# Attention times values on TensorE: four parts of 32 columns in place of two of 64

## The chip, the cores and the metric

The kernel runs on one core of a Trainium2 chip. The metric is device microseconds of one execution. A profiled execution gives, beside its time, a trace of every instruction on the engines: TensorE (PE for matmuls, PEld for its weight loads), VectorE (DVE), ScalarE (ACT), GpSimd (POOL) and SyncE (SP, which here only issues transfers).

## The reference, cut to what matters

Two blocks follow one another: an attention in which a query sees only the keys of its own hash bucket, and a feed-forward layer.

```python
# q, k, v: (4, 8, 768, 64) f32; proj: (64, 6)
q_bits = (np.einsum('bhsd,dk->bhsk', q, proj) > 0).astype(np.int64)   # k_bits alike
q_bucket = np.sum(q_bits * powers, axis=-1)                           # 64 buckets
mask = q_bucket[:, :, :, None] == k_bucket[:, :, None, :]
scores = np.where(mask, scale * np.matmul(q, k.transpose(0, 1, 3, 2)), -1000000000.0)
attn = np.exp(scores - np.max(scores, axis=-1, keepdims=True))
attn = attn / (np.sum(attn, axis=-1, keepdims=True) + 1e-09)
out = np.matmul(attn, v)                  # the change is in this product
...
x = out.transpose(0, 2, 1, 3).reshape(B * S, H * D)                   # (3072, 512)
h = x @ w_in                              # w_in (512, 2048)
g = h * (1.0 / (1.0 + np.exp(-1.702 * h)))
return (g @ w_out).astype(np.float32)     # w_out (2048, 512)
```

## The kernel before, in words

The 32 attention heads are worked off as 16 **pairs**: `pairs` holds (batch, head pair), and the two heads j = 0, 1 of a pair share every tile. S = 768 positions are T = 6 tiles of P = 128, D = 64 is the head's width, and the queries are split into two halves c = 0, 1 of HS = 384.

All score work has keys on partitions and queries along the free axis. For pair n:

- `scores(n, c, kts)` (L423 to L433): for each key tile kt one PSUM tile `ps` gets, for each head, a bfloat16 matmul of hash features (`qf`, `kf`) and a float32 matmul of `kT` and `qT`. Each contracts over the 64 rows of its head and has 128 output partitions, so both heads use one half of the array's rows each (form 64\*128 in the profile). ACT then writes exp of it to `es[c]` (L433). `es[c]` has 385 columns per key tile and head: a last column holds a tiny constant.
- `values(n, c, kts)` (L450 to L464), the function of the change: for each key tile t and head j a float32 matmul with `vt[:, t, j, :]` (128 keys x 64) as weights and `es[c][:, t, j, :]` (128 keys x 385) as the moving operand, summed over the six key tiles into partitions 64 j to 64 j + 63 of `av`. Weights of 64 columns use one half of the array's columns (form 128\*64).
- `unload` (L471): ACT moves `av` into `xT`, the transposed input of the feed-forward, and adds the last column's value.
- `hashed` (L402 to L409) projects q and k of a later pair on the hash directions: four float32 matmuls with 32 weight columns each, 128 rows contracted, 384 moving columns, into the partition quarters of one PSUM tile (form 128\*32, L408).
- `total` (L477 to L484) sums the exponentials over the partitions with a matrix of ones: four float32 matmuls of the same shape (L484), from `acc`, which POOL (L440, L441) and DVE (L446, L448) have summed over the key tiles.
- `turn` (L388 to L391) transposes a later pair's k and q into `kT` and `qT` on DVE. These have two buffers, so pair n + 2 overwrites what the scores of pair n read.

The order of the work is written out by hand (L530 to L609) for TensorE, DVE, ACT and POOL. From pair 2 on TensorE does for each pair: the scores of both halves, the values of both halves, `hashed(n + 2)`, `total(n)`. Pairs 14 and 15 have no `hashed`; pair 1 has one before its values as well; pair 0 is split into smaller pieces. Between them DVE also converts parts of `w_in` (`convert`, L158) and inverts and applies the sums (L490 to L504).

TensorE's matmuls on float32 appear in the trace as two passes, each with a weight load of its own: where the program has one instruction, the trace has two loads and two matmuls.

The feed-forward (L693 on) comes behind, first L722, then L834, with products of matrix quarters; the change does not touch it. Last there is a second version of the whole computation (L998 on) that only runs when a value is too large; it is not run here.

Of the kernel before, what the change touches and what calls it, by code (L numbers as in the profile page):

```python
# [38 lines left out]
def kernel(  # L39
# [17 lines left out]
    nc = tc.nc  # L57

    loader = [nc.sync]
    B, H, S, D = q.shape  # L60
# [3 lines left out]
    T = S // P  # L64
# [218 lines left out]
    def attention(ff):  # L283
# [4 lines left out]
        with actx:  # L288
# [11 lines left out]
            es = [ep.tile([P, T, 2, HS + 1], F32, name=f"e{i}") for i in range(2)]  # L300
# [149 lines left out]
            def values(n, c, kts):  # L450
                if 0 in kts:


                    if c and n == 0 or c and n + 2 > last:
                        avs[n, c] = mps.tile([P, HS + 1], F32, tag="m", name="av")
                    elif c:
                        avs[n, c] = sps.tile([P, 2, 512], F32, tag="s", name="av1")[:, 0, 0 : HS + 1]
                    else:
                        avs[n, c] = aps.tile([P, HS + 1], F32, tag="av", name="av")
                av, vt = avs[n, c], vts[n]  # L460
                for t in kts:
                    for j in range(2):
                        nc.tensor.matmul(av[D * j : D * (j + 1), :], vt[:, t, j, :], es[c][:, t, j, :],  # L463
                                         start=(t == 0), stop=(t == T - 1))  # L464

            def x_of(n):
                b, hp = pairs[n]
# [71 lines left out]
            turn(1, "k")  # L539
            measure(1, "k")  # L540
            values(0, 0, low)
            fetch(2, "k")
            scores(0, 1, low)
            add_low(0, 1)
            add_high(0, 0)
            turn(1, "q")
            measure(1, "q")
            values(0, 0, high)
            unload(0, 0)
            hashed(1)  # L550
# [3 lines left out]
            scores(0, 1, high)  # L554
            measure(2, "k")
            values(0, 1, low)
            values(0, 1, high)
            unload(0, 1)
# [476 lines left out]
```

## Time and profile before

| what | us |
|---|---|
| median of 4 runs | 871.52 (871.29 to 872.07) |
| the profiled execution | 872.09 |
| its span, first to last instruction | 870.3 |
| PE busy | 860.0 |
| L463, values: 768 passes, busy | 128.2 (mean of one 0.488) |
| L432, scores, float32: 768 passes, busy | 155.1 (mean 0.482) |
| L484, sums: 128 passes, busy | 13.3 (mean 0.488) |
| L408, hash: 120 passes, busy | 25.2 (mean 0.498) |
| first matmul of the feed-forward (L722) at | 318.8 |

The busy time of a group is the time in which at least one of its instructions runs, put down to the engine, so 768 passes of 0.488 us with a busy time of 128.2 us say that several run at a time. The ends of matmuls are modelled; the starts are what to read, and the distance of two starts is the pace. In a line such as "299.31 0.85 PE L484 MATMUL dn<-acc,ones 128\*32 128x384 f32 x8" the columns are the start, the duration of the merged group, engine, line, operation, output<-inputs, rows\*columns of the array, the moving operand, and how many instructions were merged. "PEldq" is the queue from which TensorE's loads and matmuls come; its semaphore instructions tell when it passed a point of the program.

### The profile page before, as it was taken

The numbers are of one execution on the slowest core, as the hardware profiler recorded it, in microseconds if no ns is written. First come the engines' busy times: TensorE is split into PE (matmuls) and PEld (weight loads), VectorE is DVE, ScalarE is ACT, GpSimd is POOL, SyncE is SP. The second block draws the span as 40 slices with busy tenths as digits, with TensorE's granted clock in tenths as the row PEclk, the third lists the DMA queues.
The fourth block names the chain that finished last, engine by engine and source line by source line (L and its number), as shares of the span: only waits on it lengthen the run. The fifth ranks groups of instructions, "written<-read, shape, count | busy, mean of one in ns | idle before, by whom it ended". The sixth has DMA issues, their size and how long they took to land.

```text
span 870.3 us, 11937 instructions
## 1 busy us (share of the span) xinstructions
PE 860.0 (99%) x4077; PEld 503.0 (58%) x4077; DVE 722.6 (83%) x1020; ACT 313.4 (36%) x519; POOL 312.6 (36%) x275
## 2 busy tenths in 40 slices
PE   9999999999999999999999999999999999999996
PEld 5444444444444444444444444444888888888885
DVE  4589999999999897778777778888888977897786
ACT  5866667777666643322233222332000000000000
POOL 4242223324323466665543344659903100000000
PEclk9999999999999999999999999999999999999998
DMA  5537544445762204555455555575844685467524
GB/s 129 92 53 116 99 87 84 84 87 109 109 99 64 62 2 177 186 206 204 176 188 184 203 182 204 185 251 175 305 163 159 198 246 198 163 207 243 194 98 99
DMA packets 169156, 132.00 MB, mean 152 GB/s; under 512 B 123616, under 2 KB 138112, under 8 KB 163712
## 3 DMA queue, kind: packets, MB, share of 16 engines
q1 hardware_dynamic: 166528, 129.70, 51.8%
q10 hardware_dynamic: 2560, 1.46, 0.8%
q8 instruction: 34, 0.56, 0.3%
q14 instruction: 34, 0.28, 0.1%
HBM read 79.69 MB, written 50.33 MB: 149 GB/s over the span
## 4 chain that ended last, share of the span: by engine, by line
PE 97%; DVE 2%; issue 0%; ACTq 0%; ACT 0%; DVEq 0%
PE product L722 33%; PE product L834 27%; PE ps L432 18%; PE av L463 15%; PE hash L408 1%; PE dn L484 1%; DVE xT L838 1%; PE tp L366 1%; DVE y L814 1%; PE warm L359 0%; PE hash L373 0%; DVE v L838 0%; DVE raw_g L220 0%; DVE t2a L221 0%; ACTq L821 0%
## 5 line engine op out<-in xcount | busy, mean ns | idle before, releaser
L433 ACT ACTIVATE e<-ps 128x768 f32<-128x768 f32 x192 | 151.3, 812 | 28.0 <-PE ps L432 25.5
L432 PE MATMUL ps<-qT,kT 64*128 64x384 f32 x768 | 155.1, 482 | 0.0
L722 PE MATMUL product<-xT,w_in_sb 128*128 128x512 f32 x288 | 135.4, 592 | 0.0
L463 PE MATMUL av<-e,v 128*64 128x385 f32 x768 | 128.2, 488 | 0.0
L440 POOL TENSOR_TENSOR acc<-e 128x768 f32<-128x768 f32 x32 | 50.3, 1573 | 197.0 <-ACT e L433 177.5
L730 ACT ACTIVATE c<-c 128x512 f32<-128x512 f32 x72 | 45.4, 630 | 186.7 <-issue 78.7
L463 PEld LDWEIGHTS av<-e,v 128*64 128x64 f32 x768 | 54.1, 136 | 71.6 <-issue 70.1
L722 PEld LDWEIGHTS product<-xT,w_in_sb 128*128 128x128 f32 x288 | 54.6, 190 | 69.0 <-issue 64.5
L432 PEld LDWEIGHTS ps<-qT,kT 64*128 64x128 f32 x768 | 68.0, 187 | 38.6 <-issue 38.5
L722 PE MATMUL product<-t_x,s_in 128*128 128x512 f32 x192 | 90.2, 592 | 0.0
L219 POOL TENSOR_TENSOR v<-c,u 128x512 f32<-128x512 f32 x24 | 34.2, 1424 | 122.8 <-ACT c L730 122.8
L847 ACT COPY u<-product 128x256 f32<-128x256 f32 x21 | 7.8, 373 | 172.1 <-PE product L834 138.9
L722 PEld LDWEIGHTS product<-t_x,s_in 128*128 128x128 f32 x192 | 36.5, 190 | 45.9 <-issue 43.3
L432 PE MATMUL ps<-qf,kf 64*128 64x384 bf16 x384 | 62.8, 324 | 0.1
L441 POOL TENSOR_TENSOR acc<-acc,e 128x768 f32<-128x768 f32 x32 | 55.7, 1741 | 2.5
L446 DVE SCALAR_TENSOR_TENSOR acc<-e 128x768 f32<-128x768 f32 x32 | 48.8, 1525 | 5.1 <-ACT e L433 5.1
L722 PE MATMUL product<-xT,s_in 128*128 128x512 f32 x96 | 45.1, 592 | 0.0
L722 PE MATMUL product<-t_x,w_in_sb 128*128 128x512 f32 x96 | 45.1, 592 | 0.0
L432 PEld LDWEIGHTS <-kf 64*128 64x128 bf16 x384 | 18.9, 94 | 35.1 <-DMA q<-in_q_dram 6.2
L448 DVE TENSOR_TENSOR acc<-acc,e 128x768 f32<-128x768 f32 x32 | 34.4, 1076 | 3.3
L834 PE MATMUL product<-raw_g,xT 128*128 128x256 f32 x152 | 35.1, 379 | 0.0
L448 DVE TENSOR_TENSOR acc<-acc,acc 128x768 f32<-128x768 f32 x32 | 31.0, 969 | 4.8 <-POOL acc L441 1.6
(207 smaller groups left out, 1499.1 us busy)
## 6 DMA issues: line engine op xcount, KB each, us to landing
raw_g<-g_dram SPq DMA_DIRECT2D x22, 1024.0 KB
s_in<-g_dram SPq DMA_DIRECT2D x20, 1024.0 KB
g_dram<-c SPq DMA_DIRECT2D x72, 256.0 KB
g_dram<-t SPq DMA_DIRECT2D x48, 256.0 KB
raw<-in_moe_w_in_dram SPq DMA_DIRECT2D x16, 512.0 KB
raw<-in_moe_w_out_dram SPq DMA_DIRECT2D x16, 512.0 KB
v<-in_v_dram SPq DMA_DIRECT2D x32, 192.0 KB
g_dram<-u SPq DMA_DIRECT2D x24, 256.0 KB
```

Of the source, the lines that this page charges most:

```text
L219: return [lambda: eng.tensor_tensor(t1, b12, b11, op=Alu.subtract), lambda: eng.tensor_tensor(b12, b22, b12, op=Alu.subtract), lambda: eng ...
L366: nc.tensor.matmul(tp[D * j : D * (j + 1), i * P : (i + 1) * P], x[name][:, j, c * GT + i, :], ident, start=True, stop=True)
L432: nc.tensor.matmul(ps[:, j, 0:HS], a[hs, keys], m[hs, cols], start=not last, stop=last)
L433: nc.scalar.activation(es[c][:, kt, :, 0:HS], ps[:, :, 0:HS], Act.Exp, scale=1.0 / D**0.5)
L440: nc.gpsimd.tensor_tensor(acc, es[c][:, 0, :, 0:HS], es[c][:, 1, :, 0:HS], op=Alu.add)
L441: nc.gpsimd.tensor_tensor(acc, acc, es[c][:, 2, :, 0:HS], op=Alu.add)
L446: nc.vector.scalar_tensor_tensor(acc, e[0], T * TINY, e[1], op0=Alu.add, op1=Alu.add)
L448: nc.vector.tensor_tensor(acc, acc, x, op=Alu.add)
L463: nc.tensor.matmul(av[D * j : D * (j + 1), :], vt[:, t, j, :], es[c][:, t, j, :], start=(t == 0), stop=(t == T - 1))
L722: nc.tensor.matmul(ps, wq[LEFT[i]][:, kc, :], xq[RIGHT[i]][:, kc, :], start=(kc == 0), stop=(kc == K2 - 1))
L730: nc.scalar.activation(c, c, Act.Gelu_apprx_sigmoid)
L834: nc.tensor.matmul(ps, wq[LEFT[i]][:, c, :], gq[RIGHT[i]][:, c, :], start=(c == 0), stop=(c == F4 - 1))
```

## The change

`values` issues, for each key tile and head, two matmuls of 32 weight columns in place of one of 64. Their outputs are the two 32-partition quarters of the head's half of `av`. The moving operand is the same for both, 385 columns; first and last key tile open and close the sum as before. Two matmuls per key tile become four, 384 become 768, in passes 768 become 1536, each with its load.

```diff
                 for t in kts:
+
                     for j in range(2):
-                        nc.tensor.matmul(av[D * j : D * (j + 1), :], vt[:, t, j, :], es[c][:, t, j, :],
-                                         start=(t == 0), stop=(t == T - 1))
+                        for d in range(0, D, 32):
+                            nc.tensor.matmul(av[D * j + d : D * j + d + 32, :], vt[:, t, j, d : d + 32], es[c][:, t, j, :],
+                                             start=(t == 0), stop=(t == T - 1))
```

The lines behind it move by two: the matmul is L465 in the kernel after, `total`'s is L486, the feed-forward's are L724 and L836.

## The prediction

> **What bounds the kernel now.** I read the page first: the busy shares (part 1) and the chain that ended last (part 4).
>
> ```profile
> PE 860.0 (99%) x4077; PEld 503.0 (58%) x4077; DVE 722.6 (83%) x1020; ACT 313.4 (36%) x519; POOL 312.6 (36%) x275
> PE 97%; DVE 2%; issue 0%; ACTq 0%; ACT 0%; DVEq 0%
> PE product L722 33%; PE product L834 27%; PE ps L432 18%; PE av L463 15%; PE hash L408 1%; PE dn L484 1%; DVE xT L838 1%; PE tp L366 1%; DVE y L814 1%; PE warm L359 0%; PE hash L373 0%; DVE v L838 0%; DVE raw_g L220 0%; DVE t2a L221 0%; ACTq L821 0%
> ```
>
> TensorE is the path, and the changed line, L463, is 15% of it. The waits view for PE lists one wait, 1.2 us at the start. So a nanosecond saved or lost between two matmuls of the attention moves the end by a nanosecond, as long as nobody else becomes late. Each float32 matmul shows as two passes: L463 has 768 records for 16 pairs x 2 halves x 6 key tiles x 2 heads = 384 matmuls.
>
> Next the PE timeline of one period, pair 13 (a period is 19.14 us):
>
> ```profile
> 272.25 7.99 PE L463 MATMUL av<-e,v 128*64 128x385 f32 x48
> 280.17 0.52 PE L408 MATMUL hash<-kT,pf_k 128*32 128x384 f32 x2
> 280.18 0.52 PE L408 MATMUL hash<-qT,pf_q 128*32 128x384 f32 x2
> 280.51 0.49 PE L408 MATMUL hash<-kT,pf_k 128*32 128x384 f32 x2
> 280.53 0.49 PE L408 MATMUL hash<-qT,pf_q 128*32 128x384 f32 x2
> 280.84 0.83 PE L484 MATMUL dn<-acc,ones 128*32 128x384 f32 x8
> 281.60 0.34 PE L432 MATMUL ps<-qf,kf 64*128 64x384 bf16 x2
> ```
>
> and the weight loads inside the value stage (columns: start, us, engine, what):
>
> ```profile
> 310.09 0.20 PEld L463 LDWEIGHTS av<-e,v 128*64 128x64 f32 x4
> 310.46 0.14 PEld L463 LDWEIGHTS av<-e,v 128*64 128x64 f32 x2 [0.18 <-issue]
> 310.79 0.14 PEld L463 LDWEIGHTS av<-e,v 128*64 128x64 f32 x2 [0.18 <-issue]
> 311.11 0.14 PEld L463 LDWEIGHTS av<-e,v 128*64 128x64 f32 x2 [0.18 <-issue]
> ```
>
> The reader is to see three things. The 64-column parts already run two at a time: every 0.323 us a group of two starts. Lines L408 and L484 are already what the change makes of L463: four parts of 32 columns, 128 rows, 384 moving columns. Their four matmuls start within 0.02 us, the second passes 0.34 us later, and dn follows hash after 0.32 us. And between the last value group and hash there is more: the instruction starts give 0.426 us from the last L463 group (279.742) to the first L408 matmul (280.168).
>
> **The change, part by part.**
>
> *The pace inside the stage: no change.* Per key tile, 4 passes two at a time are 2 groups; 8 passes four at a time are 2 groups too. A group of two with 385 columns takes 0.323 us, a group of four with 384 columns 0.322 (hash to dn). 192 key tiles x 2 groups, 0 us each. Each load of 32 columns takes 0.109 us (L408), of 64 columns 0.136 (L463); both lie under a group, so the shorter load gains nothing here. So the naive gain of twice the parallelism is nothing: half of the array's columns was never idle.
>
> *The switch of tile shape behind the stage: gone.* Wherever consecutive stages have different shapes (64\*128, 128\*64, 128\*32, 128\*128), the last matmul to the next start is 0.41 us: 0.412 scores to av, 0.414 av to hash or dn, 0.42 dn to scores. Where the shape stays (hash to dn) it is 0.303, group start to group start 0.323. With 32 columns av, hash and dn have one shape. By group starts 0.426 becomes 0.323: 0.103 us. The value stage is followed by hash in pairs 0 to 13 and by dn in pairs 14 and 15: 16 x 0.103 = 1.65 us. In pair 1 hash also runs ahead of the value stage; that switch goes too: 0.11 us.
>
> *The first load behind a switch.* A stage that follows a switch waits for its first weights: dn takes 0.785 us to the next stage after av (pair 14), 0.761 after hash; 0.024 us. Saved 16 times: 0.38 us. At the start of the value stage the second group comes 0.374 us after the first with 64 columns; after the same switch from the scores, dn of pair 0 with 32 columns shows 0.347: 0.027 us less, in 17 starts 0.46 us; in pair 1, without the switch, 0.05 us.
>
> *Added work.* 384 more matmuls, that is 768 more loads and 768 more passes on PE's queue; the planned order of all other engines stays as it was, and no wait is added. A group of four starts 0.02 us deep in place of 0.012, so where scores follow av directly (twice, in pair 0) some 0.01 us is lost each: 0.03 us.
>
> Sum: 1.65 + 0.11 + 0.38 + 0.46 + 0.05 - 0.03 = 2.6 us less. The profiled execution took 872.09 us, 870.3 of them its span, so it would be 869.5; the median of the runs shown is 871.52, 0.57 below it, so I say 871.52 - 2.6 = **868.9 us**, 0.30% less. About 0.2%, 1.74 us, is what a measurement of this kernel can tell from no change.
>
> *What is late next.* A period gets 0.103 + 0.024 + 0.027 = 0.154 us shorter. DVE has in it:
>
> ```profile
> 213.92 0.96 DVE L448 TENSOR_TENSOR acc<-acc,acc 128x768 f32<-128x768 f32 x1
> 214.95 0.98 DVE L391 STREAM_TRANSPOSE kT<-k 128x768 f32<-128x768 f32 x1
> 215.85 0.94 DVE L391 STREAM_TRANSPOSE qT<-q 128x768 f32<-128x768 f32 x1
> ```
>
> DVE's instructions, where no semaphore instruction stands between, start some 0.08 us before the one ahead ends (215.85 against 214.95 + 0.98); only at L391 of kT, whose buffer the scores must have left, is there a gap of 0.07. So DVE waits 0.15 to 0.16 us per period for PE, just what is taken away. It stays even, or it falls behind by hundredths; its deadline, the last sum of L448 ahead of dn, ends 2.15 us before dn starts (221.27 against 223.42). Twelve periods cannot eat that. In the first feed-forward products the sum of L213 that the second product loads ends on POOL at 318.02, and that load starts at 320.18; POOL's sums hang on the scores and shift with them. Transfers for q, k and v are fetched two or three pairs ahead.
>
> *The issue rate: the unknown.* Inside the stage PE's queue must now deliver 16 instructions per key tile (8 loads, 8 passes) in 0.647 us: **40 ns each**, against 81 now. No stage of before sustains that. Bounds from rows: hash and dn together start 32 instructions in 1.01 us, 32 ns each, but from a queue that the slower value stage had filled (its semaphore instruction for dn passed at 278.14, some 34 instructions ahead of what was running). The better row is the beginning:
>
> ```profile
> L366 PEldq EVENT_SEMAPHORE  x1: 51/51/51, 3.7 to 3.7; - x1
> L373 PEldq EVENT_SEMAPHORE  x2: 51/51/51, 7.3 to 8.6; - x2
> ```
>
> Between the wait ahead of L366 (3.676) and the first wait of L373 (7.316) the queue took in all 48 loads and 48 passes of L366: 96 in 3.64 us, at most 38 ns each, and it was held back by matmuls at 53 ns each, so it can be faster. From above, the nearest row is the 51 ns of a semaphore instruction on that queue. Take 51 and a key tile costs 16 x 51 = 816 ns, +0.169 us x 192 = +32 us; take 38 and it is 0. I take 38, since it is measured on the same kind of instructions.
>
> [...]
>
> **The rivals.**
>
> A. *The queue does not keep up* (slower). For: 40 ns has never been sustained here over 16 key tiles; the 38 ns are over 96 instructions, a value stage has 384. Against: those 38 ns are an upper bound. It decides from 40 ns on: each ns above costs 16 x 192 = 3.1 us. At 51 ns: 871.5 + 32 - 2.6 = 901 us. A variant with the same sign: the queue looks only so far ahead that two parts run together once the filled queue is used up; then a tile costs 4 groups, +0.65 us x 192 = +124 us, 993 us. Hash and dn, 4 groups of four in a row, speak against it.
>
> B. *The gap is a wait, not a switch* (no change). For: the waits view puts hash's load down to DVE, "PEld hash L408 <- DVE bits L182: 7.2, 12, 0.6". Then only the shorter first loads remain, about 0.5 us: 871.0. Against: it is the same 0.60 us idle of the loads ahead of dn in pair 15, which the view calls issue; a wait for DVE would vary.
>
> C. *DVE becomes the bound.* If its 0.16 us are not slack and 2.15 us not a cushion, the twelve middle periods give nothing: 2.6 - 12 x 0.154 = 0.8 us less, 870.7.
>
> **Chances and range.** Forecast 0.74 (868.0 to 869.7: half a drain more or less, the run's own 0.3 us), B 0.05, C 0.06, A 0.15. B and C lie within 0.2%, so faster 0.74, same 0.11, slower 0.15. The range runs from 868.0 to 871.2, which takes in B and C and leaves out A, less than 2 in 10.
>
> **What would show it.** Right: the timeline has L465 with x96 per value stage of 7.78 us in place of 7.92 (23 x 0.323 + 0.347), dn always 0.76, a period of 18.99 us, loads in fours every 0.323 us, L391 of kT starting without a gap. Wrong by A: groups further apart than 0.33 us after the first two key tiles. Wrong by B: 0.41 us still stands between L465 and L408. Wrong by C: dn's loads wait for DVE's L448.

## The result, and the profile after

| | us |
|---|---|
| after, median of 40 runs | 869.83 (868.99 to 872.62) |
| before, median of 60 runs beside them | 871.40 (870.82 to 872.73) |
| ratio to before, with its 95% interval | 0.9983 [0.9979, 0.9988] |
| the profiled execution of after, and its span | 868.76, 866.9 |
| the same kernel measured twice more | 869.11 and 869.31; ratios 0.9978 [0.9968, 0.9987] and 0.9976 [0.9966, 0.9986] |

The kernel became 1.6 to 2.1 us faster by the medians, 0.17% to 0.24%, where 2.6 us were forecast. 869.83 us lies in the range, but above the forecast's own band of 868.0 to 869.7 us: the range goes on to 871.2 because it takes in rivals B and C. The two repeats lie in the band. Three things are to be separated: what the attention gained, what it lost again in one place, and what varies from run to run ahead of it.

The page of after, parts 1 and 4:

```profile
PE 856.4 (99%) x4845; PEld 499.2 (58%) x4845; DVE 719.4 (83%) x1020; ACT 313.3 (36%) x519; POOL 313.6 (36%) x275
PE 95%; DVE 3%; issue 0%; DMA 0%; ACTq 0%; ACT 0%; DVEq 0%
```

TensorE has 768 passes more and is busy 3.6 us less. The chain passes through DVE a little more often; its DVE lines are those of the feed-forward, whose first and last matmul stand 542.5 us apart in both kernels.

The PE timeline of the period of pair 13, of after:

```profile
269.39 7.97 PE L465 MATMUL av<-e,v 128*32 128x385 f32 x96
277.17 0.49 PE L408 MATMUL hash<-kT,pf_k 128*32 128x384 f32 x2
277.19 0.49 PE L408 MATMUL hash<-qT,pf_q 128*32 128x384 f32 x2
277.50 0.49 PE L408 MATMUL hash<-kT,pf_k 128*32 128x384 f32 x2
277.51 0.49 PE L408 MATMUL hash<-qT,pf_q 128*32 128x384 f32 x2
277.82 0.83 PE L486 MATMUL dn<-acc,ones 128*32 128x384 f32 x8
278.58 0.34 PE L432 MATMUL ps<-qf,kf 64*128 64x384 bf16 x2
```

By the starts the value stage takes 277.17 - 269.39 = 7.78 us (before 7.92), hash 0.65 (before 0.67), dn still 0.76. From the last matmul of L465 to hash there are now 0.298 us, before 0.414: without a change of shape the longer gap is gone. The period is 18.99 us, before 19.14.

The weight loads inside a value stage of after (start, us, engine, what; the bracket is idle time before):

```profile
306.92 0.16 PEld L465 LDWEIGHTS av<-e,v 128*32 128x32 f32 x8
307.27 0.13 PEld L465 LDWEIGHTS av<-e,v 128*32 128x32 f32 x4 [0.19 <-issue]
307.59 0.13 PEld L465 LDWEIGHTS av<-e,v 128*32 128x32 f32 x4 [0.19 <-issue]
307.92 0.13 PEld L465 LDWEIGHTS av<-e,v 128*32 128x32 f32 x4 [0.20 <-issue]
```

Loads come in fours, 0.32 us apart as the twos did, with 0.19 us of nothing between them. The pace is set by the moving columns (half of the columns take half of the time, 0.163 us, in two experiments below), and the queue keeps up.

DVE in a period of after, the lines that answer to the first two of before:

```profile
211.50 0.96 DVE L448 TENSOR_TENSOR acc<-acc,acc 128x768 f32<-128x768 f32 x1
212.54 0.98 DVE L391 STREAM_TRANSPOSE kT<-k 128x768 f32<-128x768 f32 x1
```

211.50 + 0.96 to 212.54 is 0.08 us: the gap ahead of kT, which the prediction called DVE's wait for PE and expected to close, is still there.

**The attention by itself.** From the first hash matmul (L373) to the first feed-forward matmul PE takes 309.98 us in both profiles of before and 307.51 to 307.54 in the three of after: 2.47 us less in the first of them, and nearly the same in every profile. I call this stretch the attention below and read the experiments from it, since their differences are mostly too small for medians.

### The profile page after: what moved, and what is told of

Read it like the earlier page. It is cut to its first block, busy times and chain, and to the rows that moved or that the text cites. A ratio compares the mean times of both kernels' runs of the same rounds, so it can differ in the third digit from the quotient of the medians.

```text
span 866.9 us, 13473 instructions
## 1 busy us (share of the span) xinstructions
PE 856.4 (99%) x4845; PEld 499.2 (58%) x4845; DVE 719.4 (83%) x1020; ACT 313.3 (36%) x519; POOL 313.6 (36%) x275
## 4 chain that ended last, share of the span: by engine, by line
PE 95%; DVE 3%; issue 0%; DMA 0%; ACTq 0%; ACT 0%; DVEq 0%
PE product L724 33%; PE product L836 26%; PE ps L432 18%; PE av L465 15%; PE dn L486 1%; PE hash L408 1%; DVE y L816 1%; DVE xT L840 1%; PE tp L366 0%; DVE t_x L840 0%; DMA k<-in_k_dram 0%; PE hash L373 0%; DVE t2a L221 0%; DVE raw_g L220 0%; DVE v L840 0%
## 5 line engine op out<-in xcount | busy, mean ns | idle before, releaser
L724 PE MATMUL product<-xT,w_in_sb 128*128 128x512 f32 x288 | 135.5, 593 | 0.0
L465 PE MATMUL av<-e,v 128*32 128x385 f32 x1536 | 128.0, 487 | 0.0
L724 PEld LDWEIGHTS product<-xT,w_in_sb 128*128 128x128 f32 x288 | 54.8, 190 | 68.9 <-issue 64.4
L465 PEld LDWEIGHTS av<-e,v 128*32 128x32 f32 x1536 | 48.6, 109 | 76.1 <-issue 74.5
L724 PE MATMUL product<-t_x,s_in 128*128 128x512 f32 x192 | 90.2, 593 | 0.0
L724 PEld LDWEIGHTS product<-t_x,s_in 128*128 128x128 f32 x192 | 36.6, 190 | 45.8 <-issue 43.2
L441 POOL TENSOR_TENSOR acc<-acc,e 128x768 f32<-128x768 f32 x32 | 55.9, 1746 | 2.5
L446 DVE SCALAR_TENSOR_TENSOR acc<-e 128x768 f32<-128x768 f32 x32 | 47.7, 1491 | 5.1 <-ACT e L433 5.1
L724 PE MATMUL product<-xT,s_in 128*128 128x512 f32 x96 | 45.1, 592 | 0.0
L724 PE MATMUL product<-t_x,w_in_sb 128*128 128x512 f32 x96 | 45.1, 593 | 0.0
L836 PE MATMUL product<-raw_g,xT 128*128 128x256 f32 x152 | 35.1, 379 | 0.0
```

The costliest lines, as they stand in the source:

```text
L441: nc.gpsimd.tensor_tensor(acc, acc, es[c][:, 2, :, 0:HS], op=Alu.add)
L446: nc.vector.scalar_tensor_tensor(acc, e[0], T * TINY, e[1], op0=Alu.add, op1=Alu.add)
L465: nc.tensor.matmul(av[D * j + d : D * j + d + 32, :], vt[:, t, j, d : d + 32], es[c][:, t, j, :], start=(t == 0), stop=(t == T - 1))
L724: nc.tensor.matmul(ps, wq[LEFT[i]][:, kc, :], xq[RIGHT[i]][:, kc, :], start=(kc == 0), stop=(kc == K2 - 1))
L836: nc.tensor.matmul(ps, wq[LEFT[i]][:, c, :], gq[RIGHT[i]][:, c, :], start=(c == 0), stop=(c == F4 - 1))
```

## The experiments

Theory **switch**: the pace inside a stage is the same for two parts of 64 and four of 32, and the gain comes from changes of shape between stages that go away. Rivals: **parts**, each value stage is cheaper by itself with 32 columns; **queue**, the rate of issue costs or nearly costs something; later **DVE**, the sums come too late in pair 1; and **start**, the first transfer lands later.

### Both kernels once more

No edit, beside the first two experiments on the same chip.

> The kernel before once more, as a control. Theory 'start': L373 to L722 is 309.98 us again, the first L373 matmul lies anywhere from 7.9 to 9 us. Theory 'body': the body is the one that varies. Ratio 1.000 with an interval that shows what this comparison can tell, about 0.0005 to either side.

> The changed kernel once more. Open after its first profile: that profile is 3.4 us shorter in span than the one of before, 2.47 of it from the first L373 matmul to the first feed-forward matmul and 0.85 ahead of L373, while the medians lie only 1.6 us apart. Theory 'start': the stretch ahead of L373 (8.81 us in the profile of before, 7.96 in that of after) differs from run to run, the 2.47 us behind it do not; then this profile shows 307.5 us from L373 to L724 again (within 0.1) whatever its start is, and a start anywhere from 7.9 to 9 us. Theory 'body': runs other than the profiled one lose up to 1 us in waits of the attention; then 307.5 becomes up to 308.5 in this profile, with gaps that a wait explains. Ratio to before about 0.998 in both.

Measured: before_again 871.25 us, ratio 1.0002 [0.9993, 1.0011], attention 309.98 us; after_again 869.11 us, 0.9978 [0.9968, 0.9987], attention 307.54 us. The gain is there again, and the attention repeats to 0.03 us while the point at which it starts does not: 7.61 and 9.09 us here, 8.81 and 7.96 in the first profiles.

### Only one of the two halves in parts of 32

```diff
-                        for d in range(0, D, 32):
+                    w = 32 if c else D      # second_half_32; first_half_32: D if c else 32
+                        for d in range(0, D, w):
```

> Only the products of the second query half (c = 1) are in 32-column parts, those of the first half stay at 64. Theory 'switch' (the gain is the change of tile shape between the value stage and hash or dn): the switch only moves into the middle of the value stage, from between av and hash to between the two halves; hash follows av after 0.32 us, but 0.41 us and a late second group appear between the halves. Net within 0.1 us of the kernel before from L373 to the feed-forward (309.9, before 309.98), ratio 0.9995 to 1.0005. Rival 'parts' (narrower parts are cheaper in themselves): half of the gain, 1.2 us, ratio 0.9986.

> Only the products of the first query half (c = 0) are in 32-column parts. Theory 'switch': a switch is added in the middle of the value stage of 15 pairs (0.10 us, and 0.05 for the late second group) and none is removed, except the one behind the first half of pair 0 and the one between hash and av of pair 1; the shorter first load gives 0.03 us back per pair. 15 x 0.12 - 0.3 = 1.5 us slower than before from L373 to the feed-forward (311.5), ratio 1.001 to 1.002. Rival 'parts': 1.2 us faster, ratio 0.9986.

Measured: second_half_32 871.42 us, ratio 1.0002 [0.9993, 1.0011], attention 309.96 us (0.02 less than before). first_half_32 873.51 us, 1.0026 [1.0016, 1.0036], attention 311.99 us (2.01 more). The PE timeline of pair 13 in second_half_32:

```profile
272.00 8.12 PE L465 MATMUL av<-e,v 128*64 128x385 f32 x72
279.94 0.49 PE L408 MATMUL hash<-kT,pf_k 128*32 128x384 f32 x2
```

and in first_half_32:

```profile
273.74 8.12 PE L465 MATMUL av<-e,v 128*32 128x385 f32 x72
281.79 0.52 PE L408 MATMUL hash<-kT,pf_k 128*32 128x384 f32 x2
```

The merged line carries the shape of its first matmul; inside it the shape changes once. In second_half_32 the stage takes 7.94 us: the gap ahead of hash is now 0.299 us in place of 0.414, yet the stage with its change of shape inside is 0.02 us longer than before, so what the gap lost has come back within the stage, and what hash wins (0.643 in place of 0.669 us, thirteen times) is lost there too. In first_half_32 there are two changes of shape, in the middle and ahead of hash, and the stage takes 8.05 us, 0.137 us more than before. **Parts** wanted both kernels faster, about half the gain each; it falls. **Switch** has both signs. Its size in first_half_32 was put at +1.5; of the 2.01 measured, 1.76 are switches with the late loads behind them, and 0.25 are pair 1's dn, of which more below.

### How fast can the queue deliver?

Each product is cut into 192 and 193 moving columns, so that a key tile needs twice as many loads and passes for the same columns; once with parts of 32 (pieces_32: 32 instructions per key tile), once with parts of 64 (pieces_64: 16 instructions).

```diff
-        nc.tensor.matmul(av[...], vt[...], es[c][:, t, j, :], start=(t == 0), stop=(t == T - 1))
+        for s in ((0, 192), (192, HS + 1)):
+            nc.tensor.matmul(av[..., s[0] : s[1]], vt[...], es[c][:, t, j, s[0] : s[1]],
+                             start=(t == 0 and s[0] == 0), stop=(t == T - 1 and s[0] > 0))
```

> Each product of the changed kernel is issued as two, on 192 and 193 moving columns, with the same result: 32 instructions per key tile for the same columns, 20 ns each if nothing else binds. It asks how far the queue is from its limit. Theory 'queue has room' (at most 38 ns were seen, the true limit is lower): groups of four passes every 0.163 us, a key tile 0.652 us, within 1.5 us of the changed kernel. If the limit is r ns per instruction between 20 and 38, a key tile costs 32 x r: at 30 ns 0.96 us, +60 us; at 38 ns 1.22 us, +109 us. Rival 'queue at its limit' (the changed kernel runs right at 40 ns): 1.28 us, +121 us.

> The control: parts of 64 columns as before, each product issued on 192 and 193 moving columns: 16 instructions per key tile as in the changed kernel, 40 ns each, two at a time. All theories of the queue that let the changed kernel run at 40 ns expect no stall: a key tile 4 groups x 0.163 = 0.652 us against 0.647, +1 us over the kernel before. A load of 64 columns takes 0.136 us and must fit under a group of 0.163; if it does not, the groups are 0.2 us apart and the kernel some 30 us slower.

Measured: pieces_32 872.05 us, ratio 1.0009 [0.9999, 1.0018], attention 310.05 us, 2.54 more than after. pieces_64 874.83 us, 1.0039 [1.0025, 1.0052], attention 312.21 us, 2.23 more than before. The PE timeline of pair 13 in pieces_32:

```profile
272.41 8.14 PE L466 MATMUL av<-e,v 128*32 128x192 f32 x192
280.27 0.52 PE L408 MATMUL hash<-kT,pf_k 128*32 128x384 f32 x2
280.34 0.53 PE L408 MATMUL hash<-qT,pf_q 128*32 128x384 f32 x2
280.59 0.52 PE L408 MATMUL hash<-kT,pf_k 128*32 128x384 f32 x2
280.66 0.53 PE L408 MATMUL hash<-qT,pf_q 128*32 128x384 f32 x2
```

The stage takes 7.86 us with 32 x 12 = 384 instructions, 192 loads and as many passes: 20 ns each, and it is only 0.07 us longer than with half as many. Groups start every 0.163 us in both kernels, so no group waits for the queue. The queue can be driven at twice the rate that the change needs, and rival A of the prediction was far off.

Both kernels cost more than expected, though: pieces_32 was to stay within 1.5 us of after and pieces_64 to cost 1 us. In pieces_64 all of it is in the value stages (8.05 us in place of 7.92). In pieces_32 half of it is behind them: hash's four matmuls start over 0.10 to 0.11 us where in after they start within 0.026, and dn takes 0.84 to 0.86 us in place of 0.77. This spread arises inside the value stage. The four starts of a group lie 0.04 us apart at its beginning and 0.10 from about the twentieth group on, and hash and dn, with no change of shape between, show that spread too. It isn't a sign of a queue that has run empty: dn's semaphore instruction passes with some 36 loads and passes still to start, by the same count 38 in before and 42 in after. And pieces_64, at half the rate, shows such a spread too, from 0.013 to 0.068 us for the two of a group; there hash stands behind a change of shape, and its lines L408 on kT and on qT start 0.01 us apart (281.59 and 281.60), where pieces_32 has 0.07 (280.27 and 280.34). Why the spread grows is not shown.

### One value stage in place of two

In pair 0, the kernel after does the values of the first half in two stages of three key tiles. Here they are one.

```diff
-            values(0, 0, low)
...
-            values(0, 0, high)
+            values(0, 0, every)
```

> The changed kernel with the two value pieces of the first half of pair 0 put together: the piece ahead of the scores of the second half is dropped and all six key tiles come behind them. Theory 'switch': one stage with two switches of shape less, some 0.2 us less than the changed kernel from L373 to the feed-forward (307.3) if ACT, which then gets six score tiles in a row, keeps up; the ratio to before is one or two parts in 10,000 lower than the changed kernel's, which the times can hardly tell. Rival: the piece covers PE while ACT empties the score tiles, and its place becomes a wait: 307.5 or more.

Measured: 869.52 us, ratio 0.9979 [0.997, 0.9988]; attention 307.28 us, 0.25 less than after. One stage less is two changes of shape less, for which 0.2 us were expected, and ACT's six score tiles in a row bring no new wait (the scores start every 0.81 us): this agrees with **switch**. In the median it is lost.

### Covering the late transfer

In the first four profiles with 32-column parts throughout, the last packet of the first k transfer ended at 3.50 to 3.57 us, in the five others at 3.17 to 3.29, and L366 began 0.1 to 0.4 us later. To see whether this is what the medians lack, TensorE gets a fifth warm-up matmul, which bridges that gap, in before, in after and in one_value_stage; and after is run a third time.

```diff
-                for _ in range(4):
+                for _ in range(5):
                     nc.tensor.matmul(aps.tile([P, 512], F32, tag="av", name="warm"), ...)
```

> The kernel before with five warm-up matmuls (L359) in place of four; nothing else. The fifth takes some 0.63 us, so TensorE goes on until 4.35 us, past the 4.0 to 4.1 us at which the first k transfer is awaited in the kernels with 32-column parts everywhere. Theory 'start' (the first k lands 0.27 us later in those kernels, at 3.5 us in place of 3.25, and that is part of why the medians gain less than the attention does): L366 starts at 4.35 us in place of 3.78, the attention takes its 309.98 us, and the time is 0 to 0.6 us more than before, 871.2 to 871.9. Rival 'body' (the start is the same, and outside the profile the attention gains only 1.6 to 2.1 us): says the same of this kernel alone; the pair of this one with the next tells them apart.

> The kernel after with five warm-up matmuls in place of four; nothing else. Theory 'start': the late k is covered, L366 starts at 4.35 us as in the partner with 64-column parts, and the two medians now differ by the whole 2.4 to 2.5 us of the attention (ratio 0.997 between them). Rival 'body': they still differ by 1.6 to 2.1 us.

> The kernel with one value stage for pair 0's first half, and five warm-up matmuls. Theory 'start' with 'switch': 0.25 us under the kernel after with five warm-up matmuls, 307.28 us from the first hash matmul to the feed-forward. If the five matmuls let the clock come earlier or cover the late k, it is the fastest kernel here, about 868.6 us; if they only add 0.3 us, it is no better than the same kernel with four (869.5).

> The kernel after once more, beside the three others on one chip. Theory 'start': the first hash matmul between 7.6 and 9.4 us as in the runs so far, 307.51 to 307.54 us from there to the feed-forward, the first k at 3.5 us, a median 1.6 to 2.2 us under that of before. If the first k lands at 3.2 to 3.3 us this time, the late landing is chance and not the kernel's, and 'start' loses that part.

| kernel | median | ratio | L366 begins | first hash matmul | attention |
|---|---|---|---|---|---|
| before_warm | 871.25 | 0.9999 [0.999, 1.0008] | 4.29 | 8.20 | 309.98 |
| after_warm | 869.38 | 0.998 [0.9971, 0.9989] | 4.28 | 7.87 | 307.76 |
| one_stage_warm | 869.51 | 0.9979 [0.997, 0.9988] | 4.29 | 8.58 | 307.29 |
| after_third | 869.31 | 0.9976 [0.9966, 0.9986] | 3.80 | 8.00 | 307.53 |

With the gap bridged the two kernels differ by 871.25 - 869.38 = 1.87 us, no more than without. So **start** finds no support as the cause of what the medians lack; after_warm's interval against before, 1.0 to 2.5 us, is too wide to exclude it. And the fifth matmul makes nothing faster. That a clock comes, earlier or later, no view of before or after shows: the granted clock stands at 1.00 in each 2 us of their first 22. Nor is the late transfer fixed to the kernel: in after_third it ended at 3.28 us, and L366 began at 3.80, as in before. But over all fourteen profiles the eight with 32-column parts throughout have 3.28 to 3.57 us and the six others 3.14 to 3.29, so a small tendency may remain, for which no cause is shown.

after_warm shows something else: its attention is 0.22 to 0.24 us longer than in the three profiles of after. All of that stands in one place, dn of pair 1.

### DVE in pair 1

The PE timeline and the DVE timeline at dn of pair 1, before (PE first):

```profile
51.16 0.83 PE L484 MATMUL dn<-acc,ones 128*32 128x384 f32 x8
```

```profile
49.95 0.96 DVE L448 TENSOR_TENSOR acc<-acc,acc 128x768 f32<-128x768 f32 x1
```

and after:

```profile
49.84 0.93 PE L486 MATMUL dn<-acc,ones 128*32 128x384 f32 x8
```

```profile
48.92 0.96 DVE L448 TENSOR_TENSOR acc<-acc,acc 128x768 f32<-128x768 f32 x1
```

Before, the sum ended at 50.91, 0.25 us ahead of dn. After, it ends at 49.88, when dn, which needs it for its third and fourth matmul, has begun at 49.84. Those two start 0.09 and 0.10 us after the first in place of 0.013 and 0.020, and the stage takes 0.865 us in place of 0.761; in after_again 0.886, in after_third 0.881, in after_warm 1.106. To test it, pair 0's `norm`, which DVE does at the beginning of pair 1 and whose result only the feed-forward needs, is put behind the last sum, in the kernel of one_value_stage:

```diff
                 whole(invert(n - 1))
-                norm(n - 1)
+                if n > 1:
+                    norm(n - 1)
...
                 add_high(n, 1)
+                if n == 1:
+                    norm(0)
```

> The kernel of one_value_stage in which DVE applies pair 0's sums (norm, L506, 1.57 us) behind pair 1's last L448 in place of ahead of pair 1's first L446. Theory 'DVE bound in pair 1' (with 32-column parts the sums reach TensorE too late there: dn's third and fourth matmul start 0.07 to 0.32 us late and the stage takes 0.85 to 1.11 us in place of 0.76): the last L448 ends about 1.0 us earlier, held by POOL's L441 then, dn of pair 1 takes 0.76 to 0.77 us, and the stretch from the first hash matmul to the feed-forward is 307.28 - 0.12 = 307.16 us. Rival (dn's spread comes from loads or the queue behind 96 matmuls, not from DVE): dn of pair 1 still takes 0.85 us or more, 307.28. Too small to show in the medians: 869.1 to 869.5 in either case.

Measured: 869.50 us, ratio 0.9977 [0.9966, 0.9988]; attention 307.17 us, where 307.16 was expected. DVE's timeline in norm_later, then PE's:

```profile
48.50 0.96 DVE L448 TENSOR_TENSOR acc<-acc,acc 128x768 f32<-128x768 f32 x1
49.37 1.59 DVE L506 TENSOR_TENSOR xT<-xT,rs 128x768 f32<-128x768 f32 x1
```

```profile
50.67 0.83 PE L486 MATMUL dn<-acc,ones 128*32 128x384 f32 x8
```

The sum now ends 1.2 us ahead of dn, and dn takes 0.765 us in place of 0.879. So DVE was late there, and loads or queue were not. By the attention this is the best kernel here, 2.81 us under before; by the medians it can't be told from after.

How late DVE is differs between executions. Earlier in pair 1 it transposes pair 2's q, for which it waits. In after and in after_warm:

```profile
34.56 0.98 DVE L391 STREAM_TRANSPOSE qT<-q 128x768 f32<-128x768 f32 x1 [2.23 <-DMA q<-in_q_dram]
```

```profile
35.23 0.98 DVE L391 STREAM_TRANSPOSE qT<-q 128x768 f32<-128x768 f32 x1 [2.98 <-DMA q<-in_q_dram]
```

In after, DVE then still waits 0.41 us for dn of pair 0, so q's transfer costs nothing; in after_warm it doesn't, and everything up to the last sum comes 0.25 us later, counted from the first hash matmul. The same late q (a wait of 3.20 us) stands ahead of the dn of 1.009 us in first_half_32.

## Why the prediction was right, and where it was wrong

Its terms against the starts of the stages in the first two profiles:

| term | predicted | measured |
|---|---|---|
| value stages: switch behind them, first load ahead of them, stagger, pair 1 | 1.65 + 0.46 + 0.05 - 0.03 = 2.13 | 2.125 |
| switch ahead of pair 1's values | 0.11 | 0.113 |
| first load of the stage behind | 0.38 | 0.402 |
| dn behind hash | 0 | -0.104 in pair 1, -0.070 in pairs 2 to 13 |
| sum | 2.6 | 2.47 |

- **Pace inside the stage: right.** Loads in fours every 0.32 us; second_half_32, which has 32-column parts in half of all values and gains 0.02 us, shows that the parts by themselves are worth nothing.
- **Switch and first load: right**, to some hundredths. Rival B, a gap that is a wait, falls: 0.298 us stand between values and hash, not 0.414, and the gap can be put where one likes. The loads show it too: in pair 13 hash's first load starts with its first matmul in before (280.167 and 280.168 us) and 0.32 us ahead of it in after (276.853 and 277.173). The prediction's "wherever" holds for the gap behind passes of 384 and 385 columns, 0.412 to 0.419 us in before; behind passes of 128 columns it is 0.20 us (L366 to L373, L526 to L463), and the 0.62 us behind L373 at 10.5 us hold a wait of the loads, 0.5 us, for DVE's `kf`. The "half a drain" in the forecast's band takes the gap for a draining of the array, which no run shows; they show the gap itself, 0.414 us in place of 0.298.
- **dn behind hash: a small term that was missed.** The prediction had it unchanged. In pairs 2 to 13 it takes 0.766 us in place of 0.760, 12 x 0.006 = 0.07 us; its second to fourth matmuls come less evenly, at 5 to 9, 18 to 20 and 24 to 26 ns in place of 7, 13 and 20. By the starts the value stage ahead has it already: there a group's spread grows from 20 to 26 ns. In before, hash stands behind a change of shape, and its four start within 20 ns. What makes the spread grow is not shown.
- **What is late next: wrong in place and in size.** The step read the gap of 0.07 us ahead of kT, with the 0.08 of overlap, as DVE's wait for PE. That gap did not change (0.084 to 0.074 at one pair), so it was no wait. DVE's period shrank by the same 0.15 us in another line, `norm`, L504 before and L506 after. The DVE timeline of one period of before, and POOL's beside it:

```profile
190.78 1.96 DVE L504 TENSOR_TENSOR xT<-xT,rs 128x768 f32<-128x768 f32 x1
```

```profile
190.25 1.68 POOL L441 TENSOR_TENSOR acc<-acc,e 128x768 f32<-128x768 f32 x1
```

and of after:

```profile
188.66 1.81 DVE L506 TENSOR_TENSOR xT<-xT,rs 128x768 f32<-128x768 f32 x1
```

```profile
187.98 1.68 POOL L441 TENSOR_TENSOR acc<-acc,e 128x768 f32<-128x768 f32 x1
```

  In both, DVE's instruction ends 0.81 us after POOL's does. The shortest of its 16 executions takes 0.96 us. So it looks like a short instruction that waits for POOL's, which hangs on the exponentials of ACT and so on the scores of PE: DVE's slack was hidden in the duration of an instruction, some 1.96 - 0.96 = 1.0 us per period and not 0.15. No run here moved POOL's sum away, but the traces give more than these rows: wherever L446 or `norm` starts while POOL's L441 runs, 24 to 26 times in each of the fourteen profiles, it ends 0.81 to 0.82 us after L441, whether it started 0.25 or 1.63 us ahead of that end. And where L446 starts 0.1 us ahead of L441 (once in before, at 274.21 us), it takes 0.92 us, and L441 takes 2.37 in place of 1.68. Why the one should wait for the other is not shown. The conclusion of the step, that the middle periods give their full gain, held: dn's cushion is 1.98 to 1.99 us in pairs 2 to 12 and does not shrink from pair to pair.
- **The cushion of 2.15 us: wrong for pair 1.** It was read in the middle of the kernel. In pair 1 it was 0.254 us, and PE comes 0.113 + 0.153 + 0.026 = 0.292 us earlier there; 0.254 - 0.292 = -0.04, and the sum does end 0.04 us after dn begins. The stage then lost 0.10 us, since dn's matmuls go four at a time and two of them start late. So rival C, DVE as the bound, was true in one pair of sixteen.
- **The issue rate: right, and the margin is much larger than thought.** 20 ns per instruction over a whole stage, where 38 was the bound from the trace. A load and a pass of pieces_32 take 41 ns together. The prediction's 53 ns each are counted the same way: in before the 24 passes of L366 on k take 2.59 us by the starts (3.78 to 6.37), 108 ns for a pass with its load.
- **The time.** 869.83, 869.11 and 869.31 us stand 1.57, 2.12 and 2.03 us under the medians of before beside them (871.40, 871.23, 871.34), not 2.6: 0.5 to 1.0 us are missing. In the first comparison that is clear of the noise (its interval ends at a gain of 1.8 us); the intervals of the other two reach to 2.8 and 3.0 us. 0.10 to 0.34 us are dn in pair 1, by the profiles. The rest isn't settled. In each of the fourteen profiles the time is the start, the attention and 553.15 to 553.38 us more, so only the first two can hold it. The first profile of after is no typical run: its 868.76 us lie below all 40 runs measured (868.99 and more). The profiles show that the start varies by more than what is missing: the first hash matmul came between 7.6 and 9.4 us in fourteen of them, depending on when L366's passes become fast and on when q lands, for which L366 waited 1.2 us in first_half_32. The rows of L366 in after:

```profile
L366 PE MATMUL tp<-ident,k x24: 272/417/476, 4.1 to 6.2; 128*64 128x128 f32 x24
L366 PE MATMUL tp<-ident,q x24: 272/273/323, 6.3 to 7.8; 128*64 128x128 f32 x24
```

  and in one_value_stage, where none did:

```profile
L366 PE MATMUL tp<-ident,q x24: 358/418/441, 6.7 to 9.1; 128*64 128x128 f32 x24
```

  The three numbers are the shortest, median and longest pass in ns. The mean start was 8.36 us in the six kernels with 64-column parts in them and 8.61 in the eight with 32-column parts throughout; with a spread of 1.2 and 1.6 us within each that is no difference shown. A profile takes one execution, so whether the other executions start later in the kernel after, or lose more at dn, stays open.
- **The chances.** Faster by over 0.2% had 0.74. The first comparison gives 0.17% [0.12, 0.21], the others 0.22% and 0.24%: the sign is sure, but the gain sits on the bound. The weak step is the one from the trace to the median: I gave the run's start 0.3 us, and in the profiles it has some 1.8. A spread alone doesn't move a median, so where the missing 0.5 to 1.0 us are stays open. That 869.83 us lies in the range at all is owed to its width, which was meant for B and C.

## What to carry to other kernels

Splitting a product into more, narrower parts gave nothing by itself here, where two parts of 64 columns ran at a time already (a group every 0.32 us with either width); what it gave is the shape of the neighbouring stages, so that the longer gap between them went (0.298 us in place of 0.414), and then all stages in a row had to have it: half of the change was worth nothing or cost 2 us. Look for the bound of the next engine in the shallowest place of the kernel (here pair 1, 0.25 us) and not in its middle, and look for its slack in instructions that take longer than the same ones elsewhere, not only in the gaps. Where a gain is a few tenths of a per cent, compare a stretch of the trace that repeats to hundredths of a microsecond, and expect the median to show it less exactly.

## What the runs showed of the hardware that was not expected

- TensorE's queue delivered 384 instructions in 7.86 us, 20 ns each, and the stage took 1% longer than with 192.
- The passes of L366 became fast (421 to 273 ns) between 5.3 and 8.7 us from the start of the span, and in one run not before 9.1, with TensorE at work from 1.19 us in before, in after and in that run. A fifth warm-up matmul, 0.5 us more work ahead of them, left the median where it was (ratio 0.9999 [0.999, 1.0008]).
- DVE's L446 and L504 (L506), 0.92 to 0.96 us at their shortest, ended 0.81 us after POOL's sum (L441) where that had started first, and so took up to 2.4 us; L504 shrank by the 0.15 us by which the period did.
